# Reciprocal, product and store of the softmax sums moved one burst later, and the low halves subtracted ahead of the tail copies

## Chip, cores, metric

One core of a Trainium2 chip. The metric is the device time of one execution in microseconds (us). PE is the matmul engine, PEld its weight loads, DVE the vector engine, ACT the scalar engine, POOL GpSimd, SP the engine that issues nearly all DMAs of this kernel from one queue.

## What is computed

Pooled attention for 8 batches and 8 heads (1152 keys, 576 pooled queries, head size 64), and a mixing block on its output:

```python
q_pool = q.reshape(B, H, S // 2, 2, D).mean(axis=3)
scores = np.matmul(q_pool, k.transpose(0, 1, 3, 2)) / np.sqrt(D)
scores = scores - np.max(scores, axis=-1, keepdims=True)
attn = np.exp(scores)
attn = attn / (np.sum(attn, axis=-1, keepdims=True) + 1e-09)
x = np.matmul(attn, v)            # heads side by side: (8, 576, 512)
theta = x @ w_theta
y = w_tok_r @ (x * cos(theta)) + w_tok_i @ (x * sin(theta))   # per batch, over tokens
u = x + y
out = u + np.maximum(u @ w_ch, 0.0)
```

## The kernel before

The first phase, up to about 970 us, is the attention. It runs over 32 pairs of heads (`i`), two heads side by side on the 128 partitions. float32 operands of the scores are split into a high part `hi` (rounded, by ACT) and a remainder `lo` (by DVE), and a score tile is the sum of three products and the row maximum (`nmr`), eight matmuls into a PSUM tile `pe`. The second phase, to the end, is the mixing block over 8 batches.

For each pair, in the order of its data:

- `load_q`, `load_k`, `load_v` bring `qn`, `kn`, `vn`; POOL adds the query halves (`pool_q`).
- `prep_all(i, g)` for `g` 0 and 1: PE transposes keys and queries into a PSUM tile `pt`, ACT writes `hi` from it, DVE writes `lo`. For `g` 1 ACT also copies the last queries into a block-diagonal `tail` (two copies of 64x64). `pt` comes from the PSUM tag `m`, which has two buffers.
- `maxpass`: twelve `pm` matmul groups, each in a buffer of `m`, each reduced by DVE into `mx`; `max_tail` does the same for the tail (`px`, and a corner of `pt`). `max_nm`, `max_row` and `load_max` turn the maxima into the row `nmr` (transposed by PE, copied by ACT as `mT`, placed by four small DMAs).
- `escore` computes 18 score tiles (`u` 0 and 1, `kt` 0 to 8), and ACT takes the exponential into `pc` (14 buffers). POOL adds `pc` tiles up in `ss`.
- `av(i, u)`: 36 matmuls into `pa`, then ACT copies the result to `xu`, which has two buffers.
- The normalisation: `norm_sum` (PE sums `ss` and the last `pc` over partitions, ACT adds eps: `sm`), `norm_spread` and `norm_load` (two small DMAs through DRAM, so that 1152 sums lie on 128 partitions as `rc`), `norm_recip` (DVE), `norm_save` and `norm_bcast` (DMAs to DRAM and back to all partitions as `dn`), `norm_out` (DVE: `xu` times `dn`), `norm_store` (DMA to `xd`, which the second phase reads as `xT`).

The order is written by hand. `plan(i)` gives every step a position; the unit is one score tile, a pair is 18 units, and the steps of all pairs are sorted by position and issued in that order on each engine:

```python
for u in range(2):
    at(base + AV_AT[u], 4, burst, i, u)      # 10.35 and 19.25 units after base = 18 * i
```

A burst is a run of 36 `pa` matmuls with what stands around it. `burst(i, 0)`, the first burst of pair i, holds `prep_all(i + 2, 1)`, `max_row(i + 1)`, the `pa` matmuls of `u` 0 and the sums of the pair before. `burst(i, 1)`, the second, holds `tail_prep(i)` (transposes of `g` 0 for pair i + 3, `max_tail(i + 2)`, `hi` and `lo`) and the `pa` matmuls of `u` 1. So while pair i is in its scores, DVE reduces maxima for pair i + 2, and the normalisation belongs to pair i - 1. Between these steps the conversion of the float weights runs as `wgen`, a piece at a time, on DVE, ACT and POOL.

Where two engines read one PSUM tile, the program makes the second wait for the first, in the order in which the steps are written.

Of the kernel before, what the change touches and what calls it, by code (L numbers as in the profile page):

```python
# [9 lines left out]
F32 = mybir.dt.float32  # L10
# [26 lines left out]
    "max_nm": -8.85,  # L37
    "norm_spread": 29.0,
    "norm_load": 29.15,
    "norm_recip": 34.0,  # L40
    "norm_save": 34.2,
    "norm_bcast": 34.75,
    "norm_out": 37.4,
    "norm_store": 37.5,
}
MAN = ("PE", "Activation", "DVE", "Pool", "SP")
BANKS = {}
# [31 lines left out]
def pooled_attention_moe_kernel(  # L79
# [11 lines left out]
    nc = tc.nc  # L91
    P = 128
# [3 lines left out]
    HALF = SQ // 2  # L96
    HT = SQ % P
# [3 lines left out]
    QP = SQ // QT  # L101
# [33 lines left out]
    def bank2(kind, name):  # L135
        return psum["now"][0].tile([P, 2, 512], F32, tag=kind, name=name, bufs=PAIRS[kind])
# [26 lines left out]
    with ExitStack() as p1:  # L163
# [7 lines left out]
        nrm = p1.enter_context(tc.tile_pool(name="nrm", bufs=1))  # L171
# [5 lines left out]
        tails = [opd.tile([P, P], F32R, name=f"tail_{n}", bufs=1) for n in range(2)]  # L177
# [7 lines left out]
        state = {}  # L185
# [32 lines left out]
        def prep(i):  # L218
            st = state[i]
            for n in ("hi", "lo"):  # L220
                st[n] = opd.tile([P, SQ + S], F32R, tag=n, name=f"{n}{i}")
            st["nmr"] = nmrs[i % 2]
# [4 lines left out]
        def prep_t(i, g):  # L227
            st = state[i]
            kn = st["kn"]
            pt = st["pt", g] = bank2("m", f"pt{g}_{i}")  # L230
            if g == 0:
                srcs = [[kn[:, t] for t in range(3 * n, 3 * n + 3)] for n in range(2)]
            else:
                qp = st["qp"]
                srcs = [[qp[:, t] for t in range(5)], [qp[:, 5]] + [kn[:, t] for t in (6, 7, 8)]]
            for n in range(2):
                c = 0
                for src in srcs[n]:
                    R = src.shape[0]
                    nc.tensor.transpose(  # L240
                        out=pt[:, n, c : c + R],
                        in_=src.rearrange("p h d -> p (h d)"),
                        identity=ident[0:R, 0:R],
                    )
                    c += R

        def prep_parts(i, g):
            st = state[i]
            c0, w = ((0, 3 * P), (Q0, 5 * QP))[g]
            return st["pt", g][:, :, 0:w], *(  # L250
                st[n][:, c0 : c0 + 2 * w].rearrange("p (b c) -> p b c", b=2) for n in ("hi", "lo")
            )

        def prep_hi(i, g):
            src, hi, lo = prep_parts(i, g)
            nc.scalar.copy(hi, src)  # L256
            if g == 1:
                st = state[i]
                tl = st["tail"] = tails[i % 2]
                c = QP - HT  # L260
                for hs in HEADS:
                    nc.scalar.copy(tl[hs, hs], st["pt", 1][hs, 1, c : c + HT])  # L262

        def prep_lo(i, g):
            src, hi, lo = prep_parts(i, g)
            nc.vector.tensor_tensor(lo, src, hi.bitcast(F32), ALU.subtract)  # L266

        HEADS = (slice(0, D), slice(D, P))
# [90 lines left out]
        def av(i, u):  # L359
            st = state[i]  # L360
            if u == 0:
                st["xu"] = nrm.tile([P, 2, HALF], F32, tag="xu", name=f"xu{i}", bufs=2)
            pa = bank2("e", f"pa{i}_{u}")
            for kt in range(KT):
                for h, hs in enumerate(HEADS):
                    nc.tensor.matmul(  # L366
                        pa[hs, 0, 0:HALF],
                        st["vn"][:, h, kt, :],
                        st["pc"][u, kt][:, h, :],
                        start=(kt == 0),  # L370
                        stop=(kt == KT - 1),
                    )
            nc.scalar.copy(st["xu"][:, u, :], pa[:, 0, 0:HALF])  # L373
# [56 lines left out]
        def burst(i, u):  # L430
            if u == 0:
                if i + 2 < NPAIR:
                    prep_all(i + 2, 1)
                px = max_row(i + 1) if i + 1 < NPAIR else bank2("m", f"pmt{i}")
                av(i, u)
                if i > 0:
                    norm_sum(i - 1, px)
            else:
                tail_prep(i)
                av(i, u)  # L440

        def prep_all(i, g):
            if g == 0:
                prep(i)
            prep_t(i, g)
            prep_hi(i, g)
            prep_lo(i, g)

        def tail_prep(i):
            more = i + 3 < NPAIR  # L450
            if more:
                prep(i + 3)
                prep_t(i + 3, 0)
            if i + 2 < NPAIR:
                max_tail(i + 2, state[i + 3]["pt", 0] if more else None)
            if more:
                prep_hi(i + 3, 0)
                prep_lo(i + 3, 0)
# [159 lines left out]
        def plan(i):  # L618
# [5 lines left out]
            if i < 3:  # L624
                at(PRO[i][0], 3, prep_all, i, 0)
            if i < 2:
                at(PRO[i][1], 3, prep_all, i, 1)
                at(PRO[i][2], 3, max_tail, i, None)
# [327 lines left out]
```

## Time and profile before

| | |
|---|---|
| median of 3 runs | 1473.13 us (1468.17 to 1479.07) |
| the profiled execution | 1473.04 us, its span 1471.3 us |
| mean granted PE clock in it | 0.982 |
| PE busy | 1370.8 us, 93% of the span |
| DVE, ACT, POOL busy | 58%, 50%, 61% |
| DMA moved | 111.66 MB, mean 76 GB/s |

The busy shares are means over two phases with different limits; a wait is worth something only if the engine that waits is the one that sets the time there. A row of a wait reads: who waited, for whom, total us, how often, the longest. A row of the time order reads: start, duration, engine, line, operation, what is written from what, and in brackets how long the engine was idle before it and what ended that. Line numbers are those of the kernel before.

### The profile page before, as it was taken

How to read it: one execution, taken by the hardware profiler on the slowest of the kernel's cores; microseconds unless marked ns; L12 is line 12 of the kernel's file. 1: busy time of each engine (PE TensorE's matmuls, PEld its weight loads, DVE VectorE, ACT ScalarE, POOL GpSimd, SP SyncE). 2: the span in 40 equal slices, each digit the busy share in tenths (PEclk: the TensorE clock that was granted, in tenths of full speed). 3: DMA queues.
4: the chain of work that ended last, by engine and by line, in shares of the span. 5: the costliest groups of instructions: out<-in, count | busy, mean ns of one | idle time of the engine just before them, and what ended most of it. 6: DMA issues, size and time to landing. Idle time of an engine off the chain costs nothing.

```text
span 1471.3 us, 29967 instructions
## 1 busy us (share of the span) xinstructions
PE 1370.8 (93%) x12178; PEld 1093.6 (74%) x12178; DVE 847.2 (58%) x1140; ACT 730.6 (50%) x1254; POOL 902.1 (61%) x671
## 2 busy tenths in 40 slices
PE   5999999998999999999999999889999999999998
PEld 3766666666666666666666666658999999999998
DVE  6765765575567666667666766354544535536342
ACT  2555555545555454645555555564544445444441
POOL 2789777877878787788788877844313224222320
PEclk8999999999999999999999999998999999999999
DMA  5243323334333342433343331240111111111111
GB/s 126 67 111 93 108 78 91 88 95 114 82 98 89 88 113 70 112 88 105 80 116 100 88 98 50 78 126 1 54 52 33 37 33 58 47 33 37 33 30 37
DMA packets 130906, 111.66 MB, mean 76 GB/s; under 512 B 95040, under 2 KB 95424, under 8 KB 130768
## 3 DMA queue, kind: packets, MB, share of 16 engines
q1 hardware_dynamic: 130592, 109.28, 27.0%
q8 instruction: 96, 1.57, 0.5%
q0 software_dynamic: 176, 0.46, 0.1%
q14 instruction: 42, 0.34, 0.1%
HBM read 88.29 MB, written 21.27 MB: 74 GB/s over the span
## 4 chain that ended last, share of the span: by engine, by line
PE 63%; DVE 13%; DMA 11%; ACT 7%; POOL 3%; issue 3%; SPq 0%; ACTq 0%; POOLq 0%; DVEq 0%
PE pa L366 16%; PE py L793 13%; PE pe L345 10%; PE pth L721 7%; DMA rd<-sm 6%; PE pr L832 5%; DVE mx L286 5%; PE pt L240 3%; ACT pc L348 3%; DMA rc<-rd 3%; PE pmt L382 2%; POOL ss L357 2%; PE pm L279 2%; PE pxn L709 1%; PE px L296 1%
## 5 line engine op out<-in xcount | busy, mean ns | idle before, releaser
L357 POOL TENSOR_TENSOR ss<-ss,pc 128x576 f32<-128x576 f32 x384 | 554.4, 1444 | 146.1 <-ACT pc L348 124.7
L348 ACT ACTIVATE pc<-pe 128x576 f32<-128x576 f32 x576 | 371.1, 651 | 107.8 <-PE pe L345 92.2
L286 DVE TENSOR_REDUCE mx<-pm 128x2 f32<-128x768 f32 x384 | 345.4, 947 | 137.4 <-PE pm L279 136.3
L366 PE MATMUL pa<-pc,vn 128*64 128x288 f32 x2304 | 301.1, 416 | 0.3 <-ACT pc L348 0.3
L793 PE MATMUL py<-wtk,Z 128*128 128x288 f32 x1728 | 244.7, 299 | 6.9 <-DVE r L738 6.9
L366 PEld LDWEIGHTS pa<-pc,vn 128*64 128x64 f32 x2304 | 162.8, 140 | 115.6 <-issue 8.7
L768 POOL TENSOR_TENSOR Z<-ab,Z 128x512 fp32r<-128x512 f32 x40 | 52.4, 1310 | 314.6 <-ACT Z L764 314.6
L793 PEld LDWEIGHTS py<-wtk,Z 128*128 128x128 f32 x1728 | 235.6, 191 | 8.7 <-DVE r L738 7.5
L345 PE MATMUL pe<-hi 64*128 64x288 f32 x1152 | 202.3, 347 | 14.0 <-ACT pc L348 5.4
L345 PEld LDWEIGHTS pe<-hi 64*128 64x128 f32 x1152 | 107.8, 183 | 91.0 <-ACT pc L348 55.8
L345 PE MATMUL pe<-hi,lo 64*128 64x288 f32 x1152 | 170.5, 292 | 0.0
L345 PE MATMUL pe<-lo,hi 64*128 64x288 f32 x1152 | 170.3, 292 | 0.0
L345 PE MATMUL pe<-nmr,oner 64*128 64x288 f32 x1152 | 169.3, 290 | 0.0
L279 PE MATMUL pm<-hi 64*128 64x384 f32 x768 | 137.7, 357 | 21.5 <-DVE mx L286 15.7
L256 ACT CAST hi<-pt 128x768 fp32r<-128x768 f32 x64 | 56.2, 878 | 120.1 <-DVE mx L306 102.9
L373 ACT COPY xu<-pa 128x288 f32<-128x288 f32 x64 | 25.6, 400 | 171.5 <-PE pa L366 171.5
L266 DVE TENSOR_TENSOR lo<-pt,hi 128x768 fp32r<-128x768 f32 x64 | 67.6, 1057 | 74.4 <-ACT tail L262 42.1
L345 PEld LDWEIGHTS pe<-lo,hi 64*128 64x128 f32 x1152 | 109.3, 186 | 0.0
L345 PEld LDWEIGHTS pe<-hi,lo 64*128 64x128 f32 x1152 | 108.7, 185 | 0.0
L345 PEld LDWEIGHTS pe<-nmr,oner 64*128 64x128 f32 x1152 | 108.6, 185 | 0.0
L832 PEld LDWEIGHTS pr<-us,wch 128*128 128x128 f32 x768 | 104.5, 188 | 1.8
L832 PE MATMUL pr<-us,wch 128*128 128x288 f32 x768 | 105.8, 295 | 0.0
(103 smaller groups left out, 1715.9 us busy)
## 6 DMA issues: line engine op xcount, KB each, us to landing
qn<-in_q_dram SPq DMA_DIRECT2D x32, 576.0 KB
kn<-in_k_dram SPq DMA_DIRECT2D x64, 288.0 KB
vn<-in_v_dram SPq DMA_DIRECT2D x32, 576.0 KB
dn<-ro SPq DMA_DIRECT2D x64, 144.0 KB
xd<-xu SPq DMA_DIRECT2D x32, 288.0 KB
xT<-xd SPq DMA_DIRECT2D x8, 1152.0 KB
out_dram<-on SPq DMA_DIRECT2D x23, 192.0 KB
out_dram<-on SPq DMA_DIRECT2D x23, 128.0 KB
```

Of the source, the lines that this page charges most:

```text
L256: nc.scalar.copy(hi, src)
L266: nc.vector.tensor_tensor(lo, src, hi.bitcast(F32), ALU.subtract)
L279: nc.tensor.matmul(pm[:, h, 0:W], hi[hs, Q0 + j * P : Q0 + (j + 1) * P], hi[hs, K0[3 * g] : K0[3 * g] + W], start=True, stop=True,)
L286: nc.vector.tensor_reduce(mx[:, j : j + 5 : 4, g : g + 1], pm[:, :, 0:W], AX.X, ALU.max)
L345: nc.tensor.matmul(pe[:, h, 0:HALF], w[hs], x[hs], start=(n == 0), stop=(n == 3))
L348: nc.scalar.activation(pcs[u, kt], pe[:, :, 0:HALF], AF.Exp, scale=SC)
L357: nc.gpsimd.tensor_tensor(st["ss", u], first, st["pc"][u, kt], ALU.add)
L366: nc.tensor.matmul(pa[hs, 0, 0:HALF], st["vn"][:, h, kt, :], st["pc"][u, kt][:, h, :], start=(kt == 0), stop=(kt == KT - 1),)
L721: nc.tensor.matmul(th, xs[:, c, j * P : (j + 1) * P], ws[:, c], start=(n == 0), stop=(n == 11))
L768: engine("zlo", b).tensor_tensor(Z[1], t, Z[0].bitcast(F32), ALU.subtract)
L793: nc.tensor.matmul(st["py", c, u][:, 0:HALF], Z[zi][:, c * P : (c + 1) * P], wtk[wi][:, kw, u * HALF : (u + 1) * HALF], start=(i == 0 and ...
L832: nc.tensor.matmul(pr[u][:, 0:HALF], wch[wi][:, c, e * P : (e + 1) * P], st["us", ui][:, c, u * HALF : (u + 1) * HALF], start=(n == 0), st ...
```

## The change

Five positions of the plan are moved, the two tail copies are written behind `prep_lo` instead of ahead of it, and `xu` gets a third buffer:

```diff
-    "norm_recip": 34.0,
-    "norm_save": 34.2,
-    "norm_bcast": 34.75,
-    "norm_out": 37.4,
-    "norm_store": 37.5,
+    "norm_recip": 37.5,
+    "norm_save": 37.6,
+    "norm_bcast": 37.7,
+    "norm_out": 46.5,
+    "norm_store": 46.6,
...
         def prep_hi(i, g):
             src, hi, lo = prep_parts(i, g)
             nc.scalar.copy(hi, src)
-            if g == 1:
-                st = state[i]
-                tl = st["tail"] = tails[i % 2]
-                c = QP - HT
-                for hs in HEADS:
-                    nc.scalar.copy(tl[hs, hs], st["pt", 1][hs, 1, c : c + HT])
+
+        def prep_tail(i):
+            st = state[i]
+            tl = st["tail"] = tails[i % 2]
+            c = QP - HT
+            for hs in HEADS:
+                nc.scalar.copy(tl[hs, hs], st["pt", 1][hs, 1, c : c + HT])
...
-                st["xu"] = nrm.tile([P, 2, HALF], F32, tag="xu", name=f"xu{i}", bufs=2)
+                st["xu"] = nrm.tile([P, 2, HALF], F32, tag="xu", name=f"xu{i}", bufs=3)
...
             prep_t(i, g)
             prep_hi(i, g)
             prep_lo(i, g)
+            if g == 1:
+                prep_tail(i)
```

The first place is DVE around the second burst of pair 4, where maxima of pair 6 (`mx6`) are reduced, `lo7` is the first remainder of pair 7, and `rc3`, `xu3`, `dn3` belong to the normalisation of pair 3. Before:

```order
L286 TENSOR_REDUCE mx6_2075<-pm6_10_2138 128x2
L406 RECIPROCAL rc3_2080<-rc3_2080 128x9
L286 TENSOR_REDUCE mx6_2075<-pm6_11_2157 128x2
L286 TENSOR_REDUCE mx6_2075<-pm6_12_2176 128x2
L305 TENSOR_REDUCE mx6_2075<-px6_2217 128x2
L306 TENSOR_REDUCE mx6_2075<-pt0_7_2210 128x1
L266 TENSOR_TENSOR lo7_2209<-pt0_7_2210,hi7_2208 128x768
L428 TENSOR_TENSOR xu3_1629<-xu3_1629,dn3_2162 128x576
L286 TENSOR_REDUCE mx6_2075<-pm6_20_2260 128x2
```

and now, with the rows of the next first burst below (its second remainder `lo7` and the first maxima of pair 7):

```order
L287 TENSOR_REDUCE mx6_2075<-pm6_10_2138 128x2
L287 TENSOR_REDUCE mx6_2075<-pm6_11_2154 128x2
L287 TENSOR_REDUCE mx6_2075<-pm6_12_2170 128x2
L306 TENSOR_REDUCE mx6_2075<-px6_2211 128x2
L307 TENSOR_REDUCE mx6_2075<-pt0_7_2204 128x1
L267 TENSOR_TENSOR lo7_2203<-pt0_7_2204,hi7_2202 128x768
L407 RECIPROCAL rc3_2080<-rc3_2080 128x9
L287 TENSOR_REDUCE mx6_2075<-pm6_20_2258 128x2
...
L267 TENSOR_TENSOR lo7_2203<-pt1_7_2395,hi7_2202 128x960
L429 TENSOR_TENSOR xu3_1627<-xu3_1627,dn3_2244 128x576
L287 TENSOR_REDUCE mx7_2469<-pm7_00_2470 128x2
```

The reciprocal has moved past four reductions and the first remainder, and the product from behind that remainder to behind the second one, a burst later.

The second place is ACT in the first burst of pair 7, with the semaphores that each instruction waits for. Before:

```order
L256 CAST hi9_2998<-pt1_9_3180 128x960 [waits PE_49]
L262 CAST tail_1_113<-pt1_9_3180 64x64 x2
L318 CAST mT8_3196<-pmt8_3194 9x128 [waits DMAHW1_49,DMAHW7_49,DMAHW0_49,PE_49]
L373 COPY xu7_3198<-pa7_0_3199 128x288 [waits DMAHW1_49,PE_49]
L391 ACTIVATE sm6_3227<-pmt8_3194,eps_70 128x288 [waits DMAHW4_49,PE_49]
```

and now:

```order
L256 CAST hi9_2992<-pt1_9_3178 128x960 [waits PE_49]
L263 CAST tail_1_113<-pt1_9_3178 64x64 [waits DVE_49]
L263 CAST tail_1_113<-pt1_9_3178 64x64
L319 CAST mT8_3194<-pmt8_3192 9x128 [waits DMAHW7_49,DMAHW0_49,PE_49]
L374 COPY xu7_3196<-pa7_0_3197 128x288 [waits DMAHW0_49,PE_49]
L392 ACTIVATE sm6_3225<-pmt8_3192,eps_70 128x288 [waits DMAHW4_49,PE_49]
```

The order on ACT is the same; the first tail copy now waits for DVE, which is the second remainder `lo9`.

The third place is SP's queue for the transfers from the sums of pair 3 on to the loads of the next first burst. Before:

```order
L396 DMA rd3_2073<-sm3_2049 4x288
L402 DMA rc3_2080<-rd3_2073 128x9
L411 DMA ro3_2155<-rc3_2080 128x9
L419 DMA dn3_2162<-ro3_2155 64x576 x2
L463 DMA xd0_82<-xu3_1629 128x576
L191 DMA qn8_2369<-in_q_dram 96x2x768
...
L326 DMA nmr_0_108<-mT6_2413 1x16x4
L201 DMA kn8_2451<-in_k_dram 128x9x64 x2
```

and now:

```order
L397 DMA rd3_2073<-sm3_2047 4x288
L403 DMA rc3_2080<-rd3_2073 128x9
L412 DMA ro3_2242<-rc3_2080 128x9
L420 DMA dn3_2244<-ro3_2242 64x576 x2
L191 DMA qn8_2367<-in_q_dram 96x2x768
...
L327 DMA nmr_0_108<-mT6_2411 1x16x4
L466 DMA xd0_82<-xu3_1627 128x576
L201 DMA kn8_2451<-in_k_dram 128x9x64 x2
```

The store of the product has moved past the load of `qn` and the four `nmr` transfers, to just ahead of the loads of `kn`. The order on PE and POOL is the same as before.

## The prediction

> **What bounds the kernel now.** First the page: the busy shares, then the chain of work that ended last.
>
> ```profile
> PE 1370.8 (93%) x12178; PEld 1093.6 (74%) x12178; DVE 847.2 (58%) x1140; ACT 730.6 (50%) x1254; POOL 902.1 (61%) x671
> PE 63%; DVE 13%; DMA 11%; ACT 7%; POOL 3%; issue 3%; SPq 0%; ACTq 0%; POOLq 0%; DVEq 0%
> ```
>
> PE carries the time, but 11% of the chain is DMA, and in this kernel no bulk load should be that late. So the second view is the busy time by stage, with the same view for line 366 alone (the matmuls that write `pa`), which counts the pairs.
>
> ```profile
> core 0: us, PE busy (x) PEld busy (x) DVE busy (x) ACT busy (x) POOL busy (x), PEclk, DMA share, GB/s
> 72.00:929.00 857.00, 795.34 (x8038) 570.98 (x8038) 556.31 (x670) 459.72 (x796) 690.35 (x506) 0.98 0.34 93
> 72.00:929.00 857.00, 273.82 (x2090) 148.00 (x2092) 0.98 0.34 93
> ```
>
> A pair issues 72 `pa` matmuls, so 2090 are 29 pairs, 857 / 29 = 29.55 us each. PE is idle for 857 - 795 = 62 us of it and runs at a mean clock of 0.98. The third view, the waits in this stretch, says who ends the idle time.
>
> ```profile
> DVE rc L406 <- DMA rc<-rd: 58.2, 27, 5.3
> DVE lo L266 <- ACT tail L262: 38.5, 21, 2.4
> PE pt L240 <- DVE mx L286: 31.5, 22, 4.3
> PE pm L279 <- DVE mx L286: 10.5, 16, 2.4
> PE pwt L562 <- DVE mx L286: 5.5, 4, 2.1
> ```
>
> Of PE's idle time 47.5 us ends with a reduction `mx` on DVE, and DVE itself waits 58.2 us for the little transfer into `rc`. One pair in order of time shows that these are one event.
>
> ```profile
> start us, us, engine line op out<-in xcount [idle before <-releaser]
> 500.65 0.96 DVE L286 TENSOR_REDUCE mx<-pm 128x2 f32<-128x768 f32 x1 [0.53 <-PE pm L279]
> ...
> 503.35 0.29 PE L345 MATMUL pe<-nmr,oner 64*128 64x288 f32 x2
> ...
> 504.35 0.22 DVE L406 RECIPROCAL rc<-rc 128x9 f32<-128x9 f32 x1 [2.74 <-DMA rc<-rd]
> 504.48 1.76 DVE L286 TENSOR_REDUCE mx<-pm 128x2 f32<-128x768 f32 x2
> ...
> 505.44 0.87 PE L240 MATMUL pt<-ident,kn 128*128 128x128 f32 x6 [1.79 <-DVE mx L286]
> ...
> 507.51 5.69 PE L366 MATMUL pa<-pc,vn 128*64 128x288 f32 x36
> ...
> 510.52 0.80 ACT L256 CAST hi<-pt 128x768 fp32r<-128x768 f32 x1 [1.67 <-DVE mx L306]
> 511.35 0.96 DVE L266 TENSOR_TENSOR lo<-pt,hi 128x768 fp32r<-128x768 f32 x1 [0.87 <-ACT hi L256]
> ...
> 512.56 0.75 DVE L428 TENSOR_TENSOR xu<-xu,dn 128x576 f32<-128x576 f32 x1
> ```
>
> DVE runs in order. At 501.6 (500.65 + 0.96) it could take the last two reductions of this stage; instead it stands 2.74 us before the 0.22 us reciprocal. Those two reductions hold both `m` PSUM buffers, so PE, whose score matmuls end at 503.64 (503.35 + 0.29), waits 1.79 us to transpose. The bound in this stage is the reciprocal's place in DVE's queue.
>
> **The change, part by part.**
>
> *The reciprocal leaves that place* and comes after the first remainder `lo` of the same burst. Without it the two reductions run from 501.6 to 503.4 (1.76 us for both), before PE asks at 503.64. So the wait goes whole, and nothing else in the pair is late there: the scores ahead of it are paced by ACT as before. I take out the rows of `pt` and `pwt`: 31.5 + 5.5 = 37 us. Where DVE is busy with weight conversions at that point a part stays; I keep 2 us: **35 us**. Bounds: 25 if a third stays, 37.
>
> *The clock.* In some bursts the matmuls after the wait run slowly, as the same view by stretches shows (the last row is an undisturbed burst).
>
> ```profile
> 144.40:150.70 6.30, 6.30 (x39) 3.30 (x38) 3.01 (x5) 0.80 (x1) 3.28 (x3) 0.73 0.50 140
> 267.10:273.50 6.40, 6.40 (x39) 3.26 (x38) 4.27 (x4) 0.80 (x1) 6.40 (x5) 0.71 0.14 53
> 357.70:363.20 5.50, 5.50 (x39) 2.89 (x38) 3.41 (x5) 1.16 (x2) 1.40 (x1) 0.83 0.23 85
> 476.90:482.50 5.60, 5.60 (x39) 2.96 (x38) 4.31 (x4) 0.80 (x1) 4.49 (x4) 0.81 0.15 53
> 507.50:513.20 5.70, 5.70 (x39) 3.00 (x38) 4.83 (x7) 2.01 (x3) 2.87 (x2) 0.80 0.17 52
> 538.80:544.20 5.40, 5.40 (x39) 2.89 (x38) 3.48 (x4) 0.80 (x1) 3.65 (x3) 0.84 0.20 73
> 521.84:526.43 4.59, 4.59 (x41) 2.57 (x44) 1.39 (x2) 1.52 (x4) 4.28 (x4) 1.00 0.03 5
> ```
>
> Six bursts take 34.9 us where six at 4.59 us take 27.5: 7.4 us, at a granted clock of 0.71 to 0.84 against 1.00. All six stand behind such a wait, so I count **7 us**; bounds 0 and 9 (the half-speed stretch also holds the transposes ahead of the burst). The Trainium skill, "TensorE: Matmul & The Clock Gate", Part 1, says that the clock halves after an idle window of about 3.4 us. By that rule a wait of 1.79 us would not do it, only the longest, 4.3 us ahead of the burst at 357.7, and this term would be 0.9 us and the forecast 6 us later. The trace disagrees: the burst at 507.5 follows a wait of 1.79 us and ran at 0.80.
>
> *The product leaves the second burst.* It stood at 512.56 ahead of the reductions of the next part, which PE's `pm` matmuls wait for (10.5 us in all). It goes behind the second remainder of the next pair's first burst. There DVE has room:
>
> ```profile
> 521.84 0.96 ACT L256 CAST hi<-pt 128x960 fp32r<-128x960 f32 x1 [0.26 <-PE pt L240]
> ...
> 522.69 0.42 ACT L262 CAST tail<-pt 64x64 fp32r<-64x64 f32 x2
> ...
> 523.14 0.26 ACT L318 CAST mT<-pmt 9x128 fp32r<-9x128 f32 x1
> ...
> 523.15 1.16 DVE L266 TENSOR_TENSOR lo<-pt,hi 128x960 fp32r<-128x960 f32 x1 [1.07 <-ACT tail L262]
> ...
> 526.47 0.40 ACT L373 COPY xu<-pa 128x288 f32<-128x288 f32 x1 [3.08 <-PE pa L366]
> ...
> 528.48 2.69 DVE L286 TENSOR_REDUCE mx<-pm 128x2 f32<-128x768 f32 x3 [4.17 <-PE pm L279]
> ```
>
> DVE idles 4.17 us before 528.48, more than a product of 0.75 to 1.7 us. So it costs nothing there and gives back most of the 10.5 us, the weight conversions keeping the rest: **7 us**; bounds 0 and 10.5.
>
> *The remainder ahead of the tail copies.* `lo` no longer waits for `tail` (38.5 us in all), but `tail` now waits for `lo`, since both read one PSUM tile and the program lets one engine at a time read it, in the order of the code. In this pair `lo` starts at about 522.8 and ends at 524.0, the tail copies end at 524.4, and `mT` comes 1.3 us later, at 524.4 to 524.7. ACT's next instruction is the copy of `xu` at 526.47, after 3.08 us of idling, so PE's burst covers it. Behind `mT` on SP's queue stand the four `nmr` transfers, and now the store of `xd`, ahead of the loads of `kn` and `vn` and of `rd`: all about 1.7 us later (1.3, and 0.33 for an issue). The margin is 1.8 us (526.47 - 524.7); a weight conversion on DVE ahead of `lo` can eat it, and no row here says in how many pairs. I charge 0.1 us a pair, **-3 us**; bounds 0 and 8. The freed DVE time itself is not on the path; the reader must not count 38.5 us.
>
> *The third `xu` buffer* adds no instruction; the copies into it stop waiting for the product of two pairs before, a wait without a row of its own: 0.
>
> *The new waits.* The reciprocal now must find `rc`, the product `dn`. The worst landing of `rc`, and the pair in which everything came early:
>
> ```profile
> 338.39 4.59 PE L366 MATMUL pa<-pc,vn 128*64 128x288 f32 x36
> ...
> 354.49 0.21 DVE L406 RECIPROCAL rc<-rc 128x9 f32<-128x9 f32 x1 [5.26 <-DMA rc<-rd]
> ...
> 727.89 4.59 PE L366 MATMUL pa<-pc,vn 128*64 128x288 f32 x36
> ...
> 740.05 0.22 DVE L406 RECIPROCAL rc<-rc 128x9 f32<-128x9 f32 x1 [1.20 <-DMA rc<-rd]
> 742.72 4.59 PE L366 MATMUL pa<-pc,vn 128*64 128x288 f32 x36
> ...
> 747.71 1.06 DVE L428 TENSOR_TENSOR xu<-xu,dn 128x576 f32<-128x576 f32 x1 [1.69 <-DMA dn<-ro]
> 755.58 1.68 PE L366 MATMUL pa<-pc,vn 128*64 128x288 f32 x12
> ```
>
> `rc` lands 12 to 16.1 us after a first burst starts (740.05 - 727.89; 354.49 - 338.39). The second burst starts 14.8 us after it (742.72 - 727.89) and `lo` ends 4.8 us further on (511.35 + 0.96 - 507.51), so the reciprocal comes at 19.6: 3.5 us to spare in the worst pair, 1.8 after the later queue. `dn` lands 7.7 us after the reciprocal (740.05 to 747.71), at 27.3; the product comes 2 us into the next first burst, at 27.7 + 2 = 29.7. Both waits: 0.
>
> Sum: 35 + 7 + 7 - 3 = 46 us. A check from another side: the pair from 727.89 to 755.58 took 27.69 us with the shortest wait of its kind (the reciprocal stood only 1.20 us). 29 x (29.55 - 27.69) = 54 us if all pairs came to that; some carry more weight conversions. I take 47. The profiled execution took 1473.04 us (span 1471.3), the median is 1473.13, so nothing is to be corrected: **1426 us**. From 929 on PE, ACT and POOL keep their order; on SP the last store of `xd` now stands ahead of the first load of `wch`, which only the channel matmuls behind the whole token stage need, so it gets no term.
>
> **The rivals.**
>
> *The gap is refilled* by the next limit. POOL is busy 690.35 of 857 us, 23.8 us a pair; at 27.9 us a pair it would be at 85%, and scores wait for buffers that its sums free. If the period stops at 28.5, the gain is 29 x 1.05 = 30 us: 1443. For it: a pair with little waiting still needs 27.7. Against: POOL has 4.1 us a pair left at the forecast.
>
> *All of it and more:* PE's whole idle time of 62 us and 9 us of clock would be 71 us, 1402, and that is a floor; the 47.5 us that end with `mx`, 9 us and no cost of the order give 1416. Between them lies 1403 to 1413.
>
> *The change does not do what it says:* something else makes the reductions late (ACT's scores, the conversions), and only the product's 7 us come, at most: 1466 to 1473. Against it stands the row at 504.35: the wait ended with the DMA, and the reductions start in the same instant.
>
> *Slower: the wait moves to the product.* It now stands ahead of the reductions that PE needs 6.64 us after a first burst starts (528.48 - 521.84), and its transfers start some 6 us later, with `qn` and `xd` close behind. `dn` due at 27.3 may come up to 27.7 + 6.64 - 1 = 33.3 before PE feels it; each us beyond costs 29 us in all, and from 1.6 us beyond (47 / 29) the kernel is slower. So it decides at a `dn` 7.6 us late; at 9 us late the price is 29 x 1.4 = 40 us: 1513, at 8 us 1485. For it: `rc` already came 4 us later in one pair than in another. Against: nothing here delayed a transfer by twice that.
>
> **How the numbers follow.** Forecast 1426 (1413 to 1440): 0.61. Refilled, 1440 to 1456: 0.17. More than forecast, 1403 to 1413: 0.08. Nothing, 1461 to 1475: 0.08. Slower, over 1488: 0.06. The range 1408 to 1452 takes the forecast, most of the refill and half of the better case: 0.79. About 1% (15 us) is what a measurement of this kernel tells from no change: faster 0.86, same 0.08, slower 0.06.
>
> **What would show it.** The wait of DVE at the reciprocal should fall from 58.2 us to under 5, PE's wait for `mx` at `pt` and `pwt` from 37 to under 5, the DMA share of the chain in this stage to almost nothing; the stretch of 29 pairs should last about 810 us and show a clock of 0.99 or 1.00. `tail` should wait for `lo` on ACT with no wait of PE behind it. I am wrong if the product shows a wait for `dn` with `pm` waiting behind it, if POOL's share nears 95%, or if PE's idle time at `pt` is there again under another releaser.

## The result, and the profile after

| | before | changed |
|---|---|---|
| median in one series | 1470.70 us (1468.17 to 1479.07, 4 runs) | 1423.31 us (1419.16 to 1425.17, 4 runs) |
| the same in a second series | 1472.03 us (1470.14 to 1480.56, 9 runs) | 1424.27 us (1422.50 to 1425.12, 5 runs) |
| profiled execution, span | 1473.04 us, 1471.3 us | 1419.16 us, 1417.4 us |

The ratio is 0.9664 with a 95% interval of 0.9618 to 0.9711, and 0.9665 (0.9638 to 0.9691) in the second series: 47 us faster, 1423 against a forecast of 1426. The two traces differ by 54 us, since the profiled execution of the changed kernel was the shortest of its four and that of the kernel before lay 2 us above its median; readings of the traces below are held against 54.

The page of the changed kernel, busy shares and the chain that ended last:

```profile
PE 1352.0 (95%) x12178; PEld 1085.4 (77%) x12178; DVE 860.3 (61%) x1140; ACT 733.2 (52%) x1254; POOL 908.3 (64%) x671
PE 70%; DVE 14%; ACT 9%; DMA 3%; issue 3%; POOL 1%; SPq 0%; ACTq 0%; POOLq 0%; DVEq 0%
```

DMA's share of the chain went from 11% to 3%, PE's from 63% to 70%. The busy time of the stage with the 29 pairs follows, and below it the same stretch for the `pa` matmuls alone, 2088 of them, which makes it the same work, to two matmuls, as 72 to 929 us before.

```profile
core 0: us, PE busy (x) PEld busy (x) DVE busy (x) ACT busy (x) POOL busy (x), PEclk, DMA share, GB/s
72.00:875.00 803.00, 776.42 (x8035) 563.17 (x8033) 567.93 (x670) 461.52 (x795) 693.40 (x504) 1.00 0.37 99
72.00:875.00 803.00, 265.99 (x2088) 144.82 (x2088) 1.00 0.37 99
```

857 us became 803, all of the 54 us; the stage behind it kept its 499 us. The 54 us are two things. PE's idle time fell from 62 to 26.6 us (803 - 776.4), 35 us. And PE's busy time for the same instructions fell from 795.3 to 776.4, 19 us, while the granted clock went from 0.98 to 1.00. The waits in this stretch (who waited, for whom, total us, times, longest):

```profile
POOL ss L358 <- ACT pc L349: 60.3, 32, 5.2
ACT tail L263 <- DVE lo L267: 49.6, 29, 4.2
...
PE pm L280 <- DVE mx L287: 4.4, 14, 0.5
PE pmt L383 <- ACT mT L319: 3.4, 6, 1.3
PE pt L240 <- DMA kn<-in_k_dram: 3.1, 5, 1.3
...
PE pwt L565 <- DVE mx L287: 0.4, 1, 0.4
```

The row of DVE waiting for `rc` (58.2 us) and that of PE waiting for `mx` at `pt` (31.5) are gone, `pwt` is at 0.4 instead of 5.5 and `pm` at 4.4 instead of 10.5. Two rows of PE are new, for `mT` at `pmt` and for `kn` at `pt`, 6.5 us together. One second burst of the changed kernel in order of time shows the reciprocal in its new place:

```profile
503.94 0.87 PE L240 MATMUL pt<-ident,kn 128*128 128x128 f32 x6
504.16 0.33 SPq L403 DMA_DIRECT2D rc<-rd  x1
505.27 4.59 PE L367 MATMUL pa<-pc,vn 128*64 128x288 f32 x36
507.61 0.96 DVE L267 TENSOR_TENSOR lo<-pt,hi 128x768 fp32r<-128x768 f32 x1 [0.87 <-ACT hi L256]
508.48 0.20 DVE L407 RECIPROCAL rc<-rc 128x9 f32<-128x9 f32 x1
```

The transfer into `rc` is issued only after PE has begun to transpose, and nobody minds: `pt` has no bracket, the burst is 4.59 us long, and the reciprocal comes 4.3 us after the issue with no wait.

All six waits for `mT` come from pairs in which a piece of weight conversion (`wf`, once `raw`) stands on DVE ahead of the remainder, such as this first burst of the changed kernel:

```profile
434.64 4.59 PE L367 MATMUL pa<-pc,vn 128*64 128x288 f32 x36
...
436.92 1.52 DVE L507 TENSOR_SCALAR wf<-ws 128x512 uint32<-128x512 uint32 x1
438.36 1.14 DVE L267 TENSOR_TENSOR lo<-pt,hi 128x960 fp32r<-128x960 f32 x1
...
439.53 0.42 ACT L263 CAST tail<-pt 64x64 fp32r<-64x64 f32 x2 [3.91 <-DVE lo L267]
439.98 0.26 ACT L319 CAST mT<-pmt 9x128 fp32r<-9x128 f32 x1
...
440.29 0.69 PE L383 MATMUL pmt<-ss,ones 128*32 128x288 f32 x8 [1.06 <-ACT mT L319]
...
443.55 1.41 SPq L201 DMA_DIRECT2D kn<-in_k_dram  x2
...
449.16 0.85 PE L240 MATMUL pt<-ident,kn 128*128 128x128 f32 x6 [0.26 <-DMA kn<-in_k_dram]
```

`lo` starts 3.7 us after the burst does, where the prediction reckoned with 1, ACT stands 3.91 us before the tail copies, and `mT` ends at 440.24, after the burst (439.23). PE waits for it, and so do the `nmr` transfers and, behind them on SP, the load of `kn`, which is then late for the next transposes. Three of the five waits for `kn` follow such a burst. The other two (1.34 and 0.48 us) do not: there `lo` is not late, but a load of weights stands on SP ahead of `kn` as well. In all pairs `kn` goes out later than before, 6.4 us after the start of the first burst instead of 4.2 (medians over the pairs of both traces).

### The profile page after: what moved, and what is told of

The parts are those of the page before. It is cut to its first block, busy times and chain, and to the rows that moved or that the text cites. A ratio compares the mean times of both kernels' runs of the same rounds, so it can differ in the third digit from the quotient of the medians.

```text
span 1417.4 us, 29907 instructions
## 1 busy us (share of the span) xinstructions
PE 1352.0 (95%) x12178; PEld 1085.4 (77%) x12178; DVE 860.3 (61%) x1140; ACT 733.2 (52%) x1254; POOL 908.3 (64%) x671
## 4 chain that ended last, share of the span: by engine, by line
PE 70%; DVE 14%; ACT 9%; DMA 3%; issue 3%; POOL 1%; SPq 0%; ACTq 0%; POOLq 0%; DVEq 0%
PE pa L367 16%; PE pe L346 15%; PE py L796 13%; PE pth L724 7%; PE pr L835 6%; DVE mx L287 5%; ACT pc L349 4%; PE pm L280 3%; PE pt L240 3%; PE pmt L383 2%; DMA kn<-in_k_dram 2%; PE pxn L712 1%; DVE lo L267 1%; DVE wf L507 1%; DVE ws L505 1%
## 5 line engine op out<-in xcount | busy, mean ns | idle before, releaser
L367 PE MATMUL pa<-pc,vn 128*64 128x288 f32 x2304 | 293.5, 409 | 0.3 <-ACT pc L349 0.3
L367 PEld LDWEIGHTS pa<-pc,vn 128*64 128x64 f32 x2304 | 159.8, 137 | 110.7 <-ACT pc L349 4.8
L358 POOL TENSOR_TENSOR ss<-pc,pc 128x576 f32<-128x576 f32 x64 | 93.7, 1464 | 2.5 <-ACT pc L349 2.5
```

Source lines behind the costliest of these rows:

```text
L358: nc.gpsimd.tensor_tensor(st["ss", u], first, st["pc"][u, kt], ALU.add)
L367: nc.tensor.matmul(pa[hs, 0, 0:HALF], st["vn"][:, h, kt, :], st["pc"][u, kt][:, h, :], start=(kt == 0), stop=(kt == KT - 1),)
```

## The experiments

| version | median, us | ratio to before, 95% interval |
|---|---|---|
| the change | 1423.31 | 0.9664 (0.9618 to 0.9711) |
| normalisation moved, tail copies as before | 1413.37 | 0.9597 (0.9558 to 0.9636) |
| the change, tail copies behind the copy of `xu` | 1413.26 | 0.9572 (0.9541 to 0.9603) |
| only `lo` ahead of the tail copies | 1550.60 | 1.0536 (1.0491 to 1.0580) |
| the same, tail copies behind the copy of `xu` | 1457.87 | 0.9887 (0.9855 to 0.9920) |
| only product and store moved | 1511.35 | 1.0257 (1.0207 to 1.0307) |
| the same, store behind `rd` and `rc` | 1473.83 | 0.9986 (0.9962 to 1.0010) |
| reciprocal only two reductions later | 1418.53 | 0.9630 (0.9583 to 0.9677) |
| product right behind the reciprocal | 1591.48 | 1.0783 (1.0739 to 1.0827) |
| normalisation moved, two result buffers | 1462.74 | 0.9902 (0.9880 to 0.9923) |
| the change, tail copies behind the copy of `xu`, store behind `rd` and `rc` | 1413.03 | 0.9565 (0.9546 to 0.9585) |
| normalisation moved, store behind `rd` and `rc` | 1413.38 | 0.9567 (0.9548 to 0.9586) |

**1. The normalisation alone.** All five positions and the third buffer, with the tail copies ahead of `lo` as before:

```diff
-    "norm_recip": 34.0,
...
+    "norm_recip": 37.5,
...
+                st["xu"] = nrm.tile([P, 2, HALF], F32, tag="xu", name=f"xu{i}", bufs=3)
```

> Only the normalisation is moved (positions and third xu buffer as in the change); the tail copies stay ahead of the remainder. If the reciprocal's place is the cause, PE's waits for mx at pt and pwt (37 us before) stay gone and the time is 1416 to 1426 us, at or a few us below the change, because mT and the loads of kn behind it are not made late (PE's waits for mT, 3.4 us, and for kn, 3.1 us, go away). Rival, the remainder's wait for the tail copies (38.5 us) carries the gain: 1440 us or more, since that wait is back.

1413.37 us (1411.97 to 1414.46), 3 us below the range that was expected and 10 us less than the change. So moving the normalisation carries more than the whole gain, and the order of the tail copies takes some back. The stretch of its 29 pairs and the wait that the order of the tail copies was to remove:

```profile
73.00:869.00 796.00, 775.86 (x8037) 563.12 (x8034) 562.16 (x670) 458.93 (x796) 694.89 (x504) 1.00 0.38 100
```

```profile
DVE lo L266 <- ACT tail L262: 38.6, 21, 2.4
```

PE's busy time is that of the change (775.9 against 776.4), its idle time 20.1 us instead of 26.6: the 6.5 us of the two new rows. DVE still waits 38.6 us for the tail copies, and it costs nothing.

The two times came from different series, so the change was timed once more, unaltered.

> The change itself once more, since the 10 us between it and the same normalisation with the tail copies in the old order (1413 us) were taken in different series. Theory (the tail order costs 10 us in the full change): 1419 to 1426 us, and PE's waits for mT at pmt and for kn at pt there again, 3 us each in 29 pairs. Rival (the 10 us are a difference of the series): 1411 to 1416 us.

1424.27 us (1422.50 to 1425.12). Its interval (0.9638 to 0.9691) stands clear of that of the last row of the table (0.9548 to 0.9586), which is version 1 with its store placed otherwise. The two rows are there again:

```profile
PE pmt L383 <- ACT mT L319: 4.2, 6, 2.0
PE pt L240 <- DMA kn<-in_k_dram: 2.4, 5, 0.8
```

This second trace also accounts for the 10 us, which the first, of the shortest execution, did not: its 29 pairs last 806 us against 796 in version 1, with PE idle for 28.4 us against 20.1 and busy for 777.6 against 775.9. Of the 8 us of idle time 6.6 are the two rows, and 1.9 are two waits at `pt` for a weight conversion on DVE.

**2. What the tail order costs.** The change in full, with the tail copies emitted later on ACT:

```diff
                 av(i, u)
+                if i + 2 < NPAIR:
+                    prep_tail(i + 2)
                 if i > 0:
                     norm_sum(i - 1, px)
...
             prep_lo(i, g)
-            if g == 1:
-                prep_tail(i)
...
```

> The change in full, but the tail copies are emitted behind ACT's copy of xu, so that ACT no longer holds mT and xu behind the remainder on DVE. Theory (the tail order costs 10 us because mT, and with it nmr, kn and rd, come late): 1408 to 1416 us, no row of PE waiting for mT at pmt, and nmr issued 3.6 us after a first burst starts in pairs where the change has 5 to 7. Rival (what costs is lo itself starting earlier or something else of the tail order): 1419 to 1425 us, as the change.

1413.26 us (1412.47 to 1414.15): the 10 us are back, with no row of PE waiting for `mT` or `kn`. The `nmr` transfers go out even earlier than was expected, in most pairs 1.1 us after the start of a first burst and at most 3.3. `lo` still stands ahead of the tail copies here. So what cost was not `lo` first, but `mT` and the copy of `xu` queued on ACT behind two copies that wait for DVE. The edit frees both at once; that it is `mT`, and `kn` behind it, rests on the two rows of PE above, and no row of PE waiting for `xu` was there in the change.

**3. The tail order alone, and why it lost 78 us.** Normalisation as before, `lo` ahead of the tail copies:

```diff
...
             prep_hi(i, g)
             prep_lo(i, g)
+            if g == 1:
+                prep_tail(i)
```

> Only the remainder is put ahead of the tail copies; the normalisation stands where it stood. If the reciprocal's place is the cause: no gain, 1468 to 1478 us, DVE's wait for rc about 58 us and PE's wait for mx at pt and pwt about 37 us as before. Rival, the remainder's wait carries the gain: 1425 to 1450 us.

1550.60 us (1549.90 to 1555.20 in 4 runs), against 1473.06 before in its series: a miss of both theories, by 70 us. Its 29 pairs, and its waits in that stretch:

```profile
73.00:1006.00 933.00, 829.52 (x8031) 593.44 (x8031) 543.46 (x669) 462.17 (x795) 683.48 (x503) 0.94 0.32 85
```

```profile
DVE rc L407 <- DMA rc<-rd: 106.1, 29, 5.9
...
PE pt L240 <- DVE mx L287: 71.0, 25, 4.9
PE pwt L565 <- DVE mx L287: 9.7, 4, 3.4
```

DVE's wait at the reciprocal is 106.1 us instead of 58.2, PE's at `pt` and `pwt` 80.7 instead of 37. The same pair of the kernel before (first rows) and of this version (second) in order of time says why:

```profile
552.31 4.59 PE L366 MATMUL pa<-pc,vn 128*64 128x288 f32 x36
...
553.61 0.26 ACT L318 CAST mT<-pmt 9x128 fp32r<-9x128 f32 x1
...
559.09 0.57 SPq L396 DMA_DIRECT2D rd<-sm  x1
...
564.26 0.21 DVE L406 RECIPROCAL rc<-rc 128x9 f32<-128x9 f32 x1 [0.88 <-DMA rc<-rd]
...
565.34 0.88 PE L240 MATMUL pt<-ident,kn 128*128 128x128 f32 x6
```

```profile
598.54 4.59 PE L367 MATMUL pa<-pc,vn 128*64 128x288 f32 x36
...
601.17 0.26 ACT L319 CAST mT<-pmt 9x128 fp32r<-9x128 f32 x1
...
606.97 0.57 SPq L397 DMA_DIRECT2D rd<-sm  x1
...
612.21 0.21 DVE L407 RECIPROCAL rc<-rc 128x9 f32<-128x9 f32 x1 [2.60 <-DMA rc<-rd]
...
613.29 0.88 PE L240 MATMUL pt<-ident,kn 128*128 128x128 f32 x6 [1.65 <-DVE mx L287]
```

Counted from the start of the burst, `mT` starts at 1.3 us before and at 2.6 here, and `rd`, which stands behind it on SP, is issued at 6.8 and at 8.4. The reciprocal comes at 12.0 and at 13.7, and its wait grows by the same 1.7 us, from 0.88 to 2.60; PE, which did not wait in this pair, waits 1.65. This pair is typical: over all pairs of the two traces the reciprocal comes 1.7 us later on average, 14.6 us after the start of the first burst instead of 12.9. In its old place the reciprocal already waits for `rc` in 27 of 29 pairs, so a delay in that queue is passed on to it, and from it to the two reductions that PE needs. The control takes away the lateness of `mT`, with the edit of experiment 2:

> The normalisation wholly as before and the remainder ahead of the tail copies, as in the run that took 1551 us, but the tail copies are emitted behind ACT's copy of xu, so that mT is early again. Theory (that run lost because mT and with it nmr, kn, vn and rd came late, and the reciprocal waited longer for rc): the 80 us of loss go: 1462 to 1480 us, DVE's wait at the reciprocal 55 to 62 us. Rival (lo ahead of the tail copies loses by itself, for instance by the new order on DVE): 1520 us or more.

```profile
73.00:909.00 836.00, 786.98 (x8034) 566.50 (x8031) 550.52 (x670) 455.83 (x795) 689.98 (x504) 0.99 0.35 95
```

1457.87 us (1451.45 to 1470.60): not only is the loss gone, the kernel is 1.1% (0.8 to 1.5%) faster than before, and below the range that was expected. With the tail copies out of the way `mT` comes earlier than before (0.85 us after the start of the burst instead of 1.30, medians over the pairs), DVE's wait for `rc` is 45.8 us, where 55 to 62 was expected, and PE's waits at `pt` and `pwt` fall from 37 to 23.6 us (19.4 + 4.2). The queue to the reciprocal is the cause.

**4. Product and store alone.** Reciprocal and tail copies as before, three result buffers:

```diff
-    "norm_out": 37.4,
-    "norm_store": 37.5,
+    "norm_out": 46.5,
+    "norm_store": 46.6,
```

> Only the product and its store are moved (with the third xu buffer); reciprocal, its save and its spread stay. If the sum of the prediction is right, this is its third term alone: 5 to 10 us, 1461 to 1468 us; PE's wait for mx at pt and pwt stays near 37 us and bursts at half clock remain, PE's wait for mx at pm falls from 10.5 us to about 4. Rival, the product's place is the larger part: 1445 us or less.

1511.35 us (1505.01 to 1514.48), a second miss of both theories: 2.6% slower than before, where the prediction gave this part 7 us of gain. In order of time and in its 29 pairs:

```profile
547.19 1.40 SPq L463 DMA_DIRECT2D xd<-xu  x1
548.69 1.42 SPq L201 DMA_DIRECT2D kn<-in_k_dram  x2
```

```profile
73.00:964.00 891.00, 814.89 (x8033) 584.93 (x8029) 551.22 (x669) 459.83 (x795) 685.81 (x504) 0.95 0.33 89
```

```profile
DVE rc L406 <- DMA rc<-rd: 80.2, 28, 5.0
...
PE pt L240 <- DVE mx L286: 51.2, 24, 4.0
...
PE pwt L562 <- DVE mx L286: 6.2, 3, 2.3
```

The store of `xd` now stands on SP ahead of `kn`, `vn` and `rd`; the wait for `rc` grows to 80.2 us. With only the store put behind `rd` and `rc`:

```diff
-    "norm_store": 46.6,
+    "norm_store": 47.2,
```

> The product and the store moved and three result buffers, the reciprocal in its old place, as in the run that took 1511 us, but the store of xd stands behind rd and rc on the queue instead of ahead of kn. Theory (that run lost because the store delays rd and rc, and the reciprocal waits for rc ahead of the two reductions): the 40 us of loss go and some of the product's 7 us come: 1461 to 1478 us, DVE's wait at the reciprocal back to 55 to 62 us. Rival (the product's new place on DVE makes the loss): 1500 us or more, the wait at the reciprocal unchanged at about 76 us.

1473.83 us (1465.74 to 1476.41), ratio 0.9986 (0.9962 to 1.0010): the loss of 38 us (1511.35 against 1473.06 in its series) is gone, so the store's place in the queue was its cause.

```profile
DVE rc L406 <- DMA rc<-rd: 59.5, 27, 5.3
```

The wait is back at its old size. What is left of the product's own gain can't be told from nothing here, though PE's wait for `mx` at `pm` fell to 4.2 us.

**5. The reciprocal two reductions later.** As experiment 1, with the reciprocal behind the two reductions but still ahead of the tail's maxima and of `lo`:

```diff
-    "norm_recip": 37.5,
-    "norm_save": 37.6,
-    "norm_bcast": 37.7,
+    "norm_recip": 36.0,
+    "norm_save": 36.1,
+    "norm_bcast": 36.2,
```

> As the kernel with the normalisation moved alone, but the reciprocal stands only two reductions later than before, just behind those that hold the two m buffers, and ahead of the tail's reductions. If it is the two reductions queued behind it that cost, DVE may go on waiting for rc (up to some 30 us) but PE's wait at pt and pwt is gone: 1416 to 1430 us. Rival, any wait of DVE for rc is passed on to PE: the wait comes back at px or pm, 1440 us or more.

1418.53 us (1416.54 to 1419.36), and DVE still waits for `rc`:

```profile
DVE rc L406 <- DMA rc<-rd: 35.0, 25, 3.8
```

There is no row of PE waiting for `mx` at `pt` any more. What DVE's wait costs depends on what is queued behind it: 35 us of waiting cost some 5 us here, once the two reductions are ahead. Those 5 us were not traced further.

**6. The price of the slower rival.** As experiment 1, with the product right behind the reciprocal:

```diff
-    "norm_out": 46.5,
-    "norm_store": 46.6,
+    "norm_out": 37.8,
+    "norm_store": 37.9,
```

> The normalisation as in the change, but the product stands right behind the reciprocal in the second burst (the store behind it); tail copies in the old order. Theory of the slower rival (the product's wait for dn is on the path when reductions stand behind it): the reciprocal starts 3.2 us after the second burst starts, dn lands 7.7 us later, so six reductions are held until about 11.7 us after that start; PE wants the third m buffer at 6.7. It waits some 5 us a pair, 145 us, and the clock falls in addition: 1500 to 1620 us, with DVE's wait for dn over 150 us. Other theory (only the reciprocal's place matters, since the third result buffer and the transfers give room): 1410 to 1430 us and no wait of PE for mx at pm over 10 us.

```profile
73.00:1048.00 975.00, 822.30 (x8037) 619.57 (x8035) 543.89 (x670) 459.43 (x796) 690.26 (x506) 0.91 0.30 82
```

```profile
DVE xu L428 <- DMA dn<-ro: 155.3, 29, 6.5
...
PE pm L279 <- DVE mx L286: 140.8, 29, 7.4
```

1591.48 us (1590.49 to 1595.03), 8% slower than before. The product waits 5.4 us a pair for `dn`, PE waits 4.9 us a pair for the reductions behind it. So the mechanism of the rival exists, and it is the product's distance from the reciprocal, 9 of the 18 units of a pair, that keeps it away.

**7. The third buffer.** As experiment 1 with `bufs=2`:

> The normalisation as in the change, tail copies in the old order (1413 us), with two result buffers instead of three. The copies of xu in a first burst then wait for the store of the pair two before, which has its product at the same place of the burst. Theory (the third buffer is needed by the product's new place): ACT's copy of xu waits for the transfer of xd, some 2 us of the product and 2 or more of the transfer, ACT's exponentials are late by 4 us a pair, 1500 us or more. Rival (the third buffer gives nothing, as the prediction's term of 0 says for time): 1410 to 1416 us.

1462.74 us (1460.88 to 1464.99): 49 us slower than with three, though less than the 1500 that was expected.

```profile
ACT xu L373 <- DMA xd<-xu: 113.5, 19, 9.0
...
PE pe L345 <- ACT xu L373: 35.3, 27, 4.4
```

ACT's copy of `xu` waits for the store of the pair two before, in 19 of 29 pairs by this row; in nine more it waits 5 to 6 us as well, which the view puts down to `pm` and `mx`. PE's scores wait for ACT behind it. The price was smaller than 4 us a pair because PE felt only 35.3 us of these waits; with them its busy time for the same matmuls is 12 us longer (788.3 us), and the two together are nearly all of the 49.

**8. The queue's order in the new place.** The store behind `rd` and `rc` (`norm_store` at 47.2), on experiment 1 and on experiment 2:

> The normalisation as in the change, tail copies in the old order (1413 us), and the store of xd behind rd and rc on the queue. Theory (rc has several us to spare in the new place): 1410 to 1415 us. Rival (the queue's order still costs): 1400 to 1408 us.

> The change with the tail copies behind ACT's copy of xu (1413 us) and, in addition, the store of xd behind rd and rc on the queue. Theory (with the reciprocal in its new place a transfer of rc has several us to spare, so the queue's order costs nothing any more): 1410 to 1415 us, no difference to the version without this edit. Rival (the loads of kn and vn, which now start 0.7 us earlier, still set something): 1400 to 1408 us.

1413.38 us (1412.87 to 1414.04) and 1413.03 us (1412.22 to 1414.35): no difference to 1413.37 and 1413.26. The same edit that saved 37 us in experiment 4 is worth nothing here.

The first of these two and the last version of experiment 4 differ in nothing but the positions of the reciprocal and its two transfers (34.0 to 34.75 against 37.5 to 37.7): 1473.83 us became 1413.38, ratios 0.9986 and 0.9567. So the place of the reciprocal, with its transfers, is by itself worth some 60 us, once the product, the store and the third buffer stand where they do not hurt.

The version to keep is experiment 1, the change without its new order of the tail copies: it beats both kernels.

## Why the prediction was right, point by point

*The bound* was named rightly. Experiments 1 and 5 show it from two sides: with the reciprocal behind the two reductions PE's waits at `pt` go, and where DVE then still waits 35 us it hardly costs. The pair of versions in experiment 8 shows it with the reciprocal moved alone.

*The reciprocal's 35 us:* 31.5 + 5.5 - 0.4 = 36.6 us of waits went. Right; the 2 us kept for the weight conversions were not needed.

*The clock's 7 us* was mis-sized. PE's busy time for the same instructions fell by 18.9 us (17.7 in the second trace of the change), outside the bounds of 0 to 9. The step counted only the six slow bursts, which is right as far as it goes (`pa`: 273.82 to 265.99 us, 7.8), but the transposes and the tail's maxima between the wait and the burst ran slowly too. The group of the tail's maxima in the stage, before and after:

```profile
L296 PE MATMUL px<-hi,tail 128*128 128x256 f32 (+1 forms) x87 | 24.1, 391 | 0.7 <-DVE wtk L151 0.6
```

```profile
L297 PE MATMUL px<-hi,tail 128*128 128x256 f32 (+1 forms) x87 | 20.6, 345 | 1.6 <-DVE wtk L151 1.6
```

Another 3.5 us are in this group alone, and 1.9 in the transposes of the keys (40.3 to 38.4 us). That places 13 of the 18.9 us; where the rest lies is open. The better measure was already on the first rows: a clock of 0.98 over 857 us is some 17 us. By the rule of the Trainium skill, "TensorE: Matmul & The Clock Gate", Part 1, that the clock halves after an idle window of about 3.4 us, the prediction worked out 0.9 us for this term. The trace does not agree: of the 26 waits at `pt` and `pwt` before, one (4.31 us) is longer than 2.6 us, and 18.9 us went with them.

*The product's 7 us:* in the changed kernel the wait at `pm` fell by 10.5 - 4.4 = 6.1 us, as forecast. As a part by itself it was not 7 us of gain but a loss of 38, or nothing with the store out of the way (experiment 4), though the wait at `pm` fell there as well. So that this term is a gain beside the reciprocal's move is read from the waits and not shown by a run.

*The tail's -3 us* was mis-sized. It costs 10 to 11 us by medians (1423.31 and 1424.27 against 1413.37), beyond the bound of 8. The mechanism named, a conversion on DVE ahead of `lo` eating the margin, is there, in six pairs with 0.2 to 1.3 us each at `pmt` (to 2.0 in the second trace). The lateness of `kn` was named in the step and not priced: it costs 3.1 us more at `pt` (2.4 in the second trace), in two of its five waits in the first trace without a conversion ahead of `lo`. The prediction's sign, that `tail` waits for `lo` with no wait of PE behind it, did not hold.

*The third buffer's 0* is right as a difference from a wait that was there before, but the buffer is what makes the product's place possible: 49 us without it.

*The new waits' 0* was right: no row of DVE waiting for `rc` or `dn` in the stretch, though SP issues `rd` and `rc` later. One wait of PE at `pm`, of 0.7 us, ends with the reciprocal itself.

*The sum.* In the first trace 37 + 19 + 6 - 7 is 55, against 54 measured there and 46 forecast; in the second 37 + 18 + 6 - 8.5 is 52.5, against 51 in the stretch, of which 49 are left in the span. The cause was foreseen; that the medians came within 1 us of the forecast gain of 47 is in part luck, since the clock was short by 11 to 12 us, the tail by 4 to 6 the other way, and the first trace, in which the gain is largest, is of the shortest execution. *Of the rivals*, the refilled gap did not come (POOL is at 693.40 of 803 us, 86%, and 694.89 of 796 without the tail order). "All of it and more", 1403 to 1413, is close to where the change stands without its new order of the tail copies (1413.4). "Slower" exists (experiment 6) but not at this distance.

## What to carry to other kernels

An instruction that waits for a small transfer belongs behind everything that the bound engine needs from the same queue; what its wait costs is then set by what still stands behind it (5 us for 35 us of waiting in experiment 5). While it stands in the wrong place, an edit that delays its transfer, on whatever engine or queue, can cost far more than it seems to: the new order of the tail copies cost 78 us there and the store 38, and after the move 10 us and nothing. So the parts of such a change must be priced in their order, and tried one by one, since a change that wins as a whole can hold a part that loses.

## What the runs showed of the hardware

A wait of PE went with a loss beyond its own length. The versions issue the same matmuls in 29 pairs, so their PE busy time can be set beside the waits for `mx` at `pt` and `pwt` (from the rows above, and for the row with the later store from the same two views of that version):

| | waits, us | PE busy, us | over 775.9 | clock |
|---|---|---|---|---|
| normalisation alone | 0.4 | 775.9 | 0 | 1.00 |
| tail order alone, `mT` early | 23.6 | 787.0 | 11 | 0.99 |
| before | 37.0 | 795.3 | 19 | 0.98 |
| product and store alone, store behind `rd` and `rc` | 37.2 | 792.1 | 16 | 0.99 |
| product and store alone | 57.4 | 814.9 | 39 | 0.95 |
| tail order alone | 80.7 | 829.5 | 54 | 0.94 |

To each microsecond of such a wait belong 0.4 to 0.7 us of extra matmul time at a lower granted clock. That is how 1.7 us of lateness in a queue became 78 us: in experiment 3 PE's waits grew by 44 us and its busy time by 34. In experiment 6 the waits are longer, 140.8 us at another place, and the surplus is 46 us, 0.3 us for each. The waits of the table are 0.2 to 4.9 us long; in the kernel before they are 1.4 us on average, and one of the 26 is longer than 2.6 us. What sets how much of the time behind a wait runs slowly was not tried.
